# A fused attention, MLP and gated-MLP kernel: the first two blocks' 4-byte attention loads whole blocks, transposes its weights and keeps running sums; constant products stand ahead of all, and conversions 1 to 6 behind attention's steps

## The chip, the cores and the metric

One Trainium2 chip, one of its cores. The metric is the device time of one execution in microseconds (us); three runs of the kernel are given, and one execution was profiled. Engines by the names that the profile uses: PE (TensorE, PEld its weight loads), DVE (VectorE), ACT (ScalarE), POOL (GpSimd), SP (SyncE, which here issues most DMAs).

## The reference

Three stages in sequence. `q`, `k`, `v` are [4, 8, 576, 64] in float32, and `f` holds forget gates per position. Cut to what is computed:

```python
scores = (q @ k^T) / 8
cum    = cumsum(log(clip(f, 1e-4, 1)))
scores = where(causal, -1e9, scores + cum[:, :, :, None] - cum[:, :, None, :])
attn   = exp(scores - max);  attn /= sum(attn) + 1e-9
x      = (attn @ v), heads merged to [4, 576, 512]
xn     = (x - mean) / sqrt(var + 1e-6) * g_ln
x      = x + relu(xn @ w_ch1) @ w_ch2            # hidden size 2048
h      = relu(x @ w_in);  u, v = halves of h
v_n    = (v - mean) / sqrt(var + 1e-6)
out    = (u * (w_spatial @ v_n + b_spatial)) @ w_out
```

The weights `w_ch1`, `w_ch2`, `w_in` and `w_out` are float64 and arrive as 8-byte words.

## The kernel before, in words

The rows of all batches (4 x 576) are cut into nine groups of 256 or fewer columns. `BLOCKS` lists the first eight as (batch, kind). Blocks 0 and 1 are kind 0: the first 128 rows of two batches each, whose attention has one 128x128 tile per head, done in 4-byte products by `attention32`. Blocks 2 and 3 are kind 1 (rows 128 to 255, `attention1`), the other four kind 2. Each block's attention yields xT, 512 features by 256 columns; `norm` subtracts the mean and forms the scale y; `mlp` runs the two products with the hidden size cut into 16 pieces j. Block 0's MLP (g = 0) works in 4-byte products with the converted weights as they are; the later ones use pairs of 2-byte halves that `make16` cuts out of the same weights once their scale is known (`squares`, `scales`).

Converting a weight piece (`load_w`, `narrow`, lines 509 to 519 and 480 to 501): `load_raw` (503) brings 1 MB of 8-byte words into one of two buffers `raw`; ScalarE forms the magnitude of the high word (495, into wt) and the scaled low word (496, into low); VectorE clamps (497), merges the sign (498, which reads raw too) and joins both (499). The next piece but one can be loaded when the ScalarE steps and line 498 are through. `PACE` holds back the magnitude step of a conversion until attention's step number `done[...]` has had its weights copied out of PSUM (348), for later conversions until a ReLU of the MLP. `RAWAT` and `CONV` are the positions on the plan's time axis at which raw loads and conversions are recorded.

`attention32` (308) handles a block in four steps p of four heads (two batches n, two heads u). Per step it loads the operands qk (two rows of decays, line 323, and two transfers of q and k, 325) and the values vr (326); TensorE forms the scores (332) into a PSUM bank; VectorE adds the mask and takes the minimum of the negated scores (335); ScalarE takes the exponential with its sum (337); VectorE turns the reciprocal sums into a diagonal matrix (343) and TensorE multiplies the weights with it (347), which transposes and scales at once; ScalarE copies the result (348); TensorE multiplies with the values (353), ScalarE copies them into xT (354). `norm` then forms the mean over the 512 features as four products with a matrix of ones and the mean of squares as four more where it gets no running sum s (577 to 605); the other blocks come with a running sum.

Every engine works through its own queue in order. The order is made by a scheduler from the recorded sequence, buffers and priorities; it is not written out by hand. SyncE's queue, through which most loads go, is one of them: a load that waits for its buffer holds back all loads behind it.

## Time and profile before

| | us |
|---|---|
| three runs | 810.55, 814.67, 816.39 |
| their median | 814.67 |
| the profiled execution | 813.44 |
| its span, first to last instruction | 811.7 |

Times in the profile count from the start of the span. Busy time is the time in which an engine works on an instruction. A 4-byte product shows as two MATMUL records. In a row of the timeline the first two numbers are start and duration, x is the number of records merged, and the bracket tells how long the engine was idle before and what released it. In a row of windows each engine has its busy time and its number of instructions, then come the granted TensorE clock (1.00 is 2.4 GHz, 0.50 is 1.2 GHz), the share of the DMA engines that was busy and the GB/s.

### The profile page before, as it was taken

How to read it: one execution, taken by the hardware profiler on the slowest of the kernel's cores; microseconds unless marked ns; L12 is line 12 of the kernel's file. 1: busy time of each engine (PE TensorE's matmuls, PEld its weight loads, DVE VectorE, ACT ScalarE, POOL GpSimd, SP SyncE). 2: the span in 40 equal slices, each digit the busy share in tenths (PEclk: the TensorE clock that was granted, in tenths of full speed). 3: DMA queues.
4: the chain of work that ended last, by engine and by line, in shares of the span. 5: the costliest groups of instructions: out<-in, count | busy, mean ns of one | idle time of the engine just before them, and what ended most of it. 6: DMA issues, size and time to landing. Idle time of an engine off the chain costs nothing.

```text
span 811.7 us, 16139 instructions
## 1 busy us (share of the span) xinstructions
PE 765.0 (94%) x5868; PEld 583.7 (72%) x5868; DVE 553.6 (68%) x1495; ACT 526.9 (65%) x1319; POOL 55.0 (7%) x83
## 2 busy tenths in 40 slices
PE   1799989899999999999999999999999999999997
PEld 1688878678887878788778888644447667667676
DVE  5657985788598979768876963778435663664734
ACT  4676876988499869658776962576325644656542
POOL 3000000110200110101011100100012000000000
PEclk9989999999999999999999999999999999999999
DMA  6558993765668995985795875651024230000101
GB/s 187 178 176 269 251 264 75 202 155 102 165 163 168 220 205 111 178 187 125 177 193 133 140 113 147 159 174 52 1 43 81 66 117 1 30 31 5 55 1 59
DMA packets 166066, 104.71 MB, mean 129 GB/s; under 512 B 106402, under 2 KB 153634, under 8 KB 165988
## 3 DMA queue, kind: packets, MB, share of 16 engines
q1 hardware_dynamic: 159800, 97.19, 48.4%
q0 software_dynamic: 5184, 4.72, 4.6%
q10 hardware_dynamic: 1004, 1.78, 0.7%
q8 instruction: 46, 0.75, 0.4%
q14 instruction: 32, 0.26, 0.1%
HBM read 64.37 MB, written 15.11 MB: 98 GB/s over the span
## 4 chain that ended last, share of the span: by engine, by line
PE 62%; DMA 15%; ACT 9%; DVE 9%; issue 3%; SPq 2%; POOL 0%; DVEq 0%; ACTq 0%; POOLq 0%
PE ph L666 13%; PE acc L651 12%; PE pb L607 8%; PE pb L608 8%; PE pb L609 8%; DMA PT<-P 5%; DMA raw<-in_moe_w_ch_dram 4%; PE av L427 3%; PE s L281 3%; DMA qk<-in_qk_dram 2%; DVE P L302 1%; PE s L651 1%; DVE sd L285 1%; ACT wt L559 1%; DMA vr<-in_v_dram 1%
## 5 line engine op out<-in xcount | busy, mean ns | idle before, releaser
L651 PE MATMUL acc<-hh,wt 128*128 128x256 f16 (+2 forms) x960 | 198.2, 298 | 2.6 <-ACT hh L671 2.6
L666 PE MATMUL ph<-xh,wt 128*128 128x256 f16 (+1 forms) x896 | 185.5, 289 | 4.1 <-DVE hl L675 4.0
L666 PEld LDWEIGHTS <-wt 128*128 128x128 f16 x1344 | 127.4, 98 | 49.2 <-issue 10.2
L651 PEld LDWEIGHTS <-wt 128*128 128x128 f16 x1344 | 129.5, 99 | 45.8 <-issue 6.8
L666 PE MATMUL ph<-xl,wt 128*128 128x256 f16 (+1 forms) x448 | 129.1, 288 | 0.0
L651 PE MATMUL acc<-hl,wt 128*128 128x256 f16 (+1 forms) x416 | 116.4, 284 | 0.0
L671 ACT ACTIVATE hh<-ph 128x256 f16<-128x256 f32 (+2 forms) x128 | 51.1, 399 | 45.2 <-PE ph L666 44.7
L246 ACT ACTIVATE P<-sd,st 128x512 f16<-128x512 f32 (+2 forms) x128 | 70.8, 587 | 8.3 <-DVE st L292 5.2
L675 DVE SCALAR_TENSOR_TENSOR hl<-ph,hh 128x256 f16<-128x256 f32 (+1 forms) x112 | 50.7, 454 | 37.1 <-ACT hh L671 36.7
L289 ACT ACTIVATE sd<-sd,st 128x384 f32<-128x384 f32 (+2 forms) x80 | 54.7, 684 | 21.9 <-DVE st L285 21.3
L302 DVE SCALAR_TENSOR_TENSOR P<-sd,st,P 128x384 f16<-128x384 f32 (+2 forms) x96 | 58.9, 632 | 8.4 <-ACT P L246 6.9
L281 PE MATMUL s<-x 68*128 68x384 f32 (+7 forms) x256 | 61.2, 356 | 1.3 <-DMA x<-decay_d 0.8
L696 POOL DMA_DIRECT2D x_d<-t x36 | 32.4, 1104 | 333.7 <-DVE t L692 178.0
L285 DVE CUSTOM_DVE_ANT_0 sd<-s,mask 128x384 f32<-128x384 f32 (+2 forms) x80 | 45.7, 580 | 7.7 <-PE s L281 6.8
L246 ACT ACTIVATE x<-qk 64x320 fp32r<-64x320 f32 (+1 forms) x64 | 41.6, 697 | 2.1 <-PE s L281 1.6
L281 PEld LDWEIGHTS s<-x 68*128 68x128 f32 (+3 forms) x256 | 37.7, 177 | 3.5 <-PE s L281 1.0
L427 PE MATMUL av<-PT,vp 128*64 128x320 f16 (+2 forms) x480 | 34.9, 274 | 5.2 <-DMA PT<-P 5.2
L947 DVE SCALAR_TENSOR_TENSOR u<-pb,wsc,u 128x288 f32<-128x288 f32 x32 | 15.9, 514 | 32.9 <-PE pb L946 32.9
L607 PE MATMUL pb<-x2h,wil 128*128 128x288 f16 (+2 forms) x144 | 37.9, 273 | 0.0
L608 PE MATMUL pb<-x2l,wih 128*128 128x288 f16 (+2 forms) x144 | 37.9, 273 | 0.0
L609 PE MATMUL pb<-x2h,wih 128*128 128x288 f16 (+2 forms) x144 | 37.9, 273 | 0.0
L427 PEld LDWEIGHTS <-vp 128*64 128x64 f16 (+1 forms) x480 | 24.8, 110 | 17.2 <-issue 10.7
(273 smaller groups left out, 1616.3 us busy)
## 6 DMA issues: line engine op xcount, KB each, us to landing
raw<-in_moe_w_ch_dram SPq DMA_DIRECT2D x32, 512.0 KB
qk<-in_qk_dram SPq DMA_DIRECT2D x32, 448.0 KB
vraw<-in_v_dram SPq DMA_DIRECT2D x5, 1024.0 KB
vr<-in_v_dram SPq DMA_DIRECT2D x16, 320.0 KB
x_d<-xT SPq DMA_DIRECT2D x9, 512.0 KB
x_d<-t POOLq DMA_DIRECT2D x36, 128.0 KB, 4.7
out_dram<-o SPq DMA_DIRECT2D x32, 144.0 KB
raw<-in_moe_w_in_dram SPq DMA_DIRECT2D x8, 512.0 KB
```

The lines of the kernel that those rows point to most:

```text
L246: self.nc.scalar.activation(out, in_, AF.Copy, scale=scale)
L281: nc.tensor.matmul(ps[: R * u + R, : c1 - c0], lhsT=x[:, lo - q0 - R * u : hi - q0], rhs=y[:, c0:c1], start=g == 0, stop=g == len(heads[u] ...
L285: nc.vector.tensor_tensor_reduce(out=sd[:M, c0:c1], in0=ps[:M, : c1 - c0], in1=mask, scale=-0.125, scalar=3e38 if n == 0 else st[:M, n - 1 ...
L289: nc.scalar.activation(sd[:M, :N], sd[:M, :N], AF.Exp, bias=st[:M, n : n + 1], scale=-1.0, accum_out=st[:M, 2:3])
L302: nc.vector.scalar_tensor_tensor(out=dl, in0=src, scalar=rs, in1=dh, op0=ALU.mult, op1=ALU.subtract)
L427: nc.tensor.matmul(pav[us, n0:W], lhsT=vp[:kr, vi, kt, us], rhs=heads[u][1][:kr, 2 * kt + pi, n0:W], start=(kt == 0 and (vi, pi) == (0, 1) ...
L607: first = mm(out, lhsT=al, rhs=bh, start=start, stop=False, **kw)
L608: mm(out, lhsT=ah, rhs=bl, start=False, stop=False, **kw)
L609: mm(out, lhsT=ah, rhs=bh, start=False, stop=stop, **kw)
L651: ins = nc.tensor.matmul(acc[m], lhsT=a, rhs=b, start=bank not in clear, stop=last and e == len(terms) - 1, skip_group_check=True)
L666: nc.tensor.matmul(ph, lhsT=a, rhs=b, start=k == e == 0, stop=k == NK - 1 and e == len(terms) - 1)
L671: relu = nc.scalar.activation(hh, ph, AF.Relu)
```

## The change

`attention32` loads a block's operands and values whole: two transfers for q and k, two for the decays and one for the values, where four steps had five each; both have one buffer where there were two. The weights are scaled on VectorE in place and then transposed on TensorE against the identity; the values are multiplied in two products of 256 columns, and the two halves of the result are copied by ScalarE and VectorE. The steps are recorded so that the values of a step follow the weights of the next. The block's running sum is formed on the way, and `norm` always takes one. 48 products of constants are recorded ahead of all. `PACE` now has seven entries and holds back both ScalarE steps of conversions 1 to 6. The forget gates are loaded in plain order of heads, so the rows by which decays are addressed change in all attentions.

```diff
-BUFS0 = dict(vr=2, qk=2, e=3, diag=2, PT=2, st=4)
+BUFS0 = dict(vr=1, qk=1, e=3, PT=2, st=4)
+WARM = 48
-RAWAT = (-1.1, -1.1)
+RAWAT = (-0.97, -0.97)
-PACE = (None, None, 2, 5, 7)
+PACE = (None, 0, 1, 2, 4, 6, 7)
...
-        for p in range(NP):
-            qk = at.tile([66, 2, 2, 2 * P], F32, tag="qk", name="qk", bufs=bufs["qk"])
-            vr = at.tile([P, 2, P], F32, tag="vr", name="vr", bufs=bufs["vr"])
...
+        qk = at.tile([66, 2, NP, 2, 2 * P], F32, tag="qk", name="qk", bufs=bufs["qk"])
+        vr = at.tile([P, 2, DM], F32, tag="vr", name="vr", bufs=bufs["vr"])
+        for n in range(2):
+            nc.sync.dma_start(out=qk[:64, n].rearrange("d p u s -> d p (u s)"), in_=self.qk0[b + n].rearrange("p d u s -> d p (u s)"))
+        for r in range(2):
+            nc.sync.dma_start(out=qk[64 + r : 65 + r].rearrange("r n p u s -> r (n p u) s"), in_=self.decay[b * H : b * H + 16, r])
+        nc.sync.dma_start(out=vr, in_=self.v[b : b + 2, :P, :].rearrange("b p d -> p b d"))
...
+            nc.vector.tensor_tensor(out=flat, in0=flat, in1=st[:, 1].unsqueeze(2).broadcast_to([P, 4, P]), op=ALU.mult)
...
-                mm(ps[:, n, u], lhsT=e[:, n, u], rhs=diag[:, n, u], start=True, stop=True, skip_group_check=True)
+                nc.tensor.transpose(ps[:, n, u], e[:, n, u], self.ident)
...
-                for u in (1, 0):
-                    mm(pav[: 64 * u + 64, 0, n], lhsT=vr[:, n, : 64 * u + 64], rhs=pt[:, n, u], start=True, stop=True, skip_group_check=True)
-            nc.scalar.activation(xT[:, p].rearrange("p (n w) -> p n w", n=2), pav[:, 0], AF.Copy)
+                mm(pav[:, n], lhsT=vr[:, n, p * P : (p + 1) * P], rhs=pt[:, n], start=True, stop=True, skip_group_check=True)
+            for u in range(2):
...
+                if u:
+                    nc.scalar.activation(dst, pav[us, :, u], AF.Copy)
+                else:
+                    nc.vector.tensor_copy(out=dst, in_=pav[us, :, u])
+            if p == 1:
+                self.xs = self.mo_sum(xT)
+            elif p == 2:
+                nc.vector.tensor_tensor(out=self.xs, in0=self.xs, in1=xT[:, 2, :], op=ALU.add)
...
         at = PACE[j] if j < len(PACE) else 2 * NP + j - len(PACE)
         if at is not None:
-            self.after(first, self.done[at])
+            for ins in first if j < len(PACE) else first[:1]:
+                self.after(ins, self.done[at])
...
-        if s is None or end:
+        if end:
             pv = self.mean(tag, *(sq[:, t] for t in range(NK)))
...
+        warm, ones = self.bank("s2"), self.ones.bitcast(BF16)
+        for i in range(WARM):
+            self.nc.tensor.matmul(warm[:, : 2 * P], lhsT=ones[:, :P], rhs=ones, start=True, stop=True)
```

Three places show what this moves. The first is SyncE's queue at the start of the program, before (ft are the gates, raw_150 and raw_153 the weight pieces 0 and 1, qk_157 and vr_158 the operands and values of the first step):

```order
L148 DMA ft_96<-in_f_dram 16x1x576
L507 DMA raw_150<-in_moe_w_ch1_dram 128x4x128
L508 DMA raw_150<-in_moe_w_ch2_dram 128x512
L507 DMA raw_153<-in_moe_w_ch1_dram 128x4x128
L508 DMA raw_153<-in_moe_w_ch2_dram 128x512
L325 DMA qk_157<-in_qk0_dram 64x2x256
L323 DMA qk_157<-decay_100 1x4x256 x2
```

and after, with qk_200 and vr_201 the operands and values of the whole first block and raw_207 and raw_210 pieces 0 and 1:

```order
L149 DMA ft_145<-in_f_dram 16x576
L323 DMA qk_200<-in_qk0_dram 64x4x512 x2
L326 DMA vr_201<-in_v_dram 128x2x512
L529 DMA raw_207<-in_moe_w_ch1_dram 128x4x128
L530 DMA raw_207<-in_moe_w_ch2_dram 128x512
L325 DMA qk_200<-decay_149 1x16x256 x2
L180 DMA decay1_d_67<-dec1_150 32x768
L529 DMA raw_210<-in_moe_w_ch1_dram 128x4x128
```

The block's operands and values went ahead of the raw pieces, and piece 1 behind the decays.

The second place is SyncE's queue later in these two blocks. Before, the values of the second block's steps (vr_351, vr_399, vr_447, vr_486) stand between pieces 4 and 5 (raw_535, raw_571):

```order
L507 DMA raw_535<-in_moe_w_ch1_dram 128x4x128
L326 DMA vr_351<-in_v_dram 128x2x128
L508 DMA raw_535<-in_moe_w_ch2_dram 128x512
L326 DMA vr_399<-in_v_dram 128x2x128
L1025 DMA x2_d_70<-xT_156 128x4x256
L507 DMA raw_571<-in_moe_w_ch1_dram 128x4x128
L326 DMA vr_447<-in_v_dram 128x2x128
L508 DMA raw_571<-in_moe_w_ch2_dram 128x512
L326 DMA vr_486<-in_v_dram 128x2x128
```

After, qk_379 and vr_380 are the second block's operands and values, and raw_369 to raw_666 are pieces 2 to 6:

```order
L530 DMA raw_369<-in_moe_w_ch2_dram 128x512
L323 DMA qk_379<-in_qk0_dram 64x4x512 x2
L325 DMA qk_379<-decay_149 1x16x256 x2
L529 DMA raw_452<-in_moe_w_ch1_dram 128x4x128
L530 DMA raw_452<-in_moe_w_ch2_dram 128x512
L529 DMA raw_527<-in_moe_w_ch1_dram 128x4x128
L530 DMA raw_527<-in_moe_w_ch2_dram 128x512
L529 DMA raw_562<-in_moe_w_ch1_dram 128x4x128
L530 DMA raw_562<-in_moe_w_ch2_dram 128x512
L326 DMA vr_380<-in_v_dram 128x2x512
L529 DMA raw_666<-in_moe_w_ch1_dram 128x4x128
```

The second block's operands stand behind piece 2, its values behind piece 5.

The third place is ScalarE's queue where the MLP of block 0 begins (sq is the square for the norm, xT<-xT,gT the scaling of the MLP's operand, hh the first ReLU). Before, conversions 4 and 5 are raw_535 and raw_571:

```order
L495 ACTIVATE wt_146<-raw_437 128x1024
L337 ACTIVATE e_493,st_495<-e_493,st_495 128x128 x4
L354 ACTIVATE xT_349<-s_392 128x256
L587 ACTIVATE sq_324<-xT_156 128x1024
L348 ACTIVATE PT_472<-ph_471 128x512
L338 ACTIVATE st_495<-st_495 128x4
L630 ACTIVATE xT_156<-xT_156,gT_64 128x256 x4
L354 ACTIVATE xT_349<-s_431 128x256
L496 ACTIVATE low_574<-raw_571 128x1024
L595 ACTIVATE y_314<-av_326,eps_65 128x256
L348 ACTIVATE PT_511<-ph_510 128x512
L495 ACTIVATE wt_146<-raw_535 128x1024
```

After, raw_666 is piece 6, raw_708 piece 7 and raw_770 piece 8:

```order
L352 ACTIVATE PT_507<-ph_506 128x512
L518 ACTIVATE wt_195<-raw_666 128x1024
L518 ACTIVATE low_669<-raw_666 128x1024
L607 ACTIVATE sq_345<-xT_199 128x1024
L360 ACTIVATE xT_378<-s_468 64x256
L650 ACTIVATE xT_199<-xT_199,gT_64 128x256 x4
L518 ACTIVATE low_711<-raw_708 128x1024
L360 ACTIVATE xT_378<-s_500 64x256
L518 ACTIVATE low_773<-raw_770 128x1024
L691 ACTIVATE hh_560<-ph_555 128x256
L518 ACTIVATE wt_195<-raw_708 128x1024
```

Conversion 6 stands ahead of the MLP's operand where conversion 3 stood, and the low words of pieces 7 and 8 ahead of the first ReLU.

## Rows read from the trace of the kernel before

**Rows 1.** The page's busy time, share of the span and instructions of each engine.

```profile
PE 765.0 (94%) x5868; PEld 583.7 (72%) x5868; DVE 553.6 (68%) x1495; ACT 526.9 (65%) x1319; POOL 55.0 (7%) x83
```

**Rows 2.** Windows of the whole core: the program's five stages, each engine's busy time.

```profile
14.40:31.20 16.80, 11.72 (x48) 10.57 (x49) 10.84 (x43) 9.43 (x36) 0.00 (x0) 1.00 0.60 167
31.20:59.30 28.10, 25.32 (x146) 20.43 (x146) 16.02 (x53) 20.90 (x64) 0.00 (x0) 0.88 0.59 186
59.30:145.10 85.80, 82.35 (x533) 70.40 (x533) 64.61 (x152) 63.47 (x141) 0.00 (x0) 0.98 0.77 213
145.10:171.00 25.90, 21.72 (x183) 17.64 (x182) 19.85 (x42) 25.82 (x52) 3.73 (x4) 0.93 0.63 166
171.00:811.70 640.70, 623.86 (x4966) 464.57 (x4964) 435.39 (x1189) 400.97 (x1020) 44.81 (x60) 0.99 0.50 111
```

**Rows 3.** Waits of PE in 59.3 to 145.1 us: total, times, longest.

```profile
PE av L399 <- DMA PT<-P: 3.5, 2, 3.0
```

**Rows 4.** Timeline of PE, 14 to 78 us.

```profile
14.39 2.04 PE L332 MATMUL acc<-qk 66*128 66x128 f32 x8 [14.39 <-DMA qk<-decay]
36.96 1.14 PE L332 MATMUL s<-qk 66*128 66x128 f32 x8 [2.19 <-DMA qk<-in_qk_dram]
37.92 2.57 PE L353 MATMUL av<-PT,vr 128*128 128x128 f32 x8
53.32 1.16 PE L347 MATMUL ph<-diag,e 128*128 128x128 f32 x8
59.35 1.89 PE L666 MATMUL ph<-xT,wt 128*128 128x256 f32 x8
61.08 1.53 PE L353 MATMUL s<-PT,vr 128*128 128x128 f32 x8
62.54 3.72 PE L666 MATMUL ph<-xT,wt 128*128 128x256 f32 x16
66.09 1.89 PE L651 MATMUL acc<-hh,wt 128*128 128x256 f32 x8
74.99 2.92 PE L529 MATMUL gram<-wt 128*128 128x128 bf16 x48
77.75 0.33 PE L212 MATMUL s<-vq,ones 128*128 128x1 f32 x2
```

**Rows 5.** Windows: 2 to 14.4 us, last column GB/s.

```profile
2.00:14.40 12.40, 0.01 (x1) 0.04 (x1) 6.62 (x15) 6.30 (x10) 5.02 (x13) 1.00 0.80 237
```

**Rows 6.** Timeline of ACT, 50 to 63 us.

```profile
50.50 1.17 ACT L496 ACTIVATE low<-raw 128x1024 int32<-128x1024 uint32 x1 [0.46 <-DMA raw<-in_moe_w_ch_dram]
53.06 0.43 ACT L337 ACTIVATE e<-e,st 128x128 f32<-128x128 f32 x1
54.61 0.41 ACT L354 ACTIVATE xT<-s 128x256 f32<-128x256 f32 x1
54.87 1.09 ACT L587 ACTIVATE sq<-xT 128x1024 f32<-128x1024 f32 x1
56.39 1.74 ACT L630 ACTIVATE xT<-xT,gT 128x256 f32<-128x256 f32 x4
```

**Rows 7.** Timeline of DVE, 0 to 56 us.

```profile
1.04 0.17 DVE L131 MEMSET ones<- 128x128 f32 x1
16.59 0.29 DVE L335 CUSTOM_DVE_ANT_0 e<-acc,mask 128x128 f32<-128x128 f32 x1 [0.66 <-PE acc L332]
51.70 1.22 DVE L498 SCALAR_TENSOR_TENSOR low<-raw,low 128x1024 uint32<-128x1024 uint32 x1 [0.72 <-ACT low L496]
54.17 0.68 DVE L497 TENSOR_SCALAR wt<-wt 128x1024 f32<-128x1024 f32 x1
54.88 1.22 DVE L499 SCALAR_TENSOR_TENSOR wt<-wt,low 128x1024 uint32<-128x1024 uint32 x1
```

**Rows 8.** The chain that ended last: start, us, what.

```profile
46.32 4.10 DMA raw<-in_moe_w_ch_dram
```

**Rows 9.** Windows: 38 to 40 us.

```profile
38.00:40.00 2.00, 2.00 (x8) 1.22 (x8) 2.00 (x9) 2.00 (x7) 0.00 (x0) 0.50 0.32 95
```

More of the change, by code (lines that the diff above doesn't have):

```diff
@@ L147, in decays @@
         for c, queue in ((0, nc.sync), (2 * H, nc.scalar)):
-            queue.dma_start(out=ft[c : c + 2 * H], in_=self.f[c : c + 2 * H].rearrange("(n h) s -> h n s", n=2))
+            queue.dma_start(out=ft[c : c + 2 * H], in_=self.f[c : c + 2 * H])
         nc.scalar.preload_act_table_set("natural_log_exp_and_others")
@@ L348, in attention32 @@
[L348 to L355 removed]
+            flat = e.rearrange("p n u w -> p (n u) w")
+            nc.vector.tensor_tensor(out=flat, in0=flat, in1=st[:, 1].unsqueeze(2).broadcast_to([P, 4, P]), op=ALU.mult)
@@ new lines, in weights, with values @@
+            return e
+        def values(p, e):
+            ps, pt = bank(tags[1]), four("PT")
+            for n, u, c in four_:
+                nc.tensor.transpose(ps[:, n, u], e[:, n, u], self.ident)
+            self.done.append(nc.scalar.activation(pt, ps, AF.Copy))
+            pav = bank(tags[2])
+            for n in range(2):
+                mm(pav[:, n], lhsT=vr[:, n, p * P : (p + 1) * P], rhs=pt[:, n], start=True, stop=True, skip_group_check=True)
+            for u in range(2):
+                us = slice(64 * u, 64 * u + 64)
+                dst = xT[us, p].rearrange("p (n w) -> p n w", n=2)
+                if u:
[6 more added lines that the diff above has]
+                nc.vector.tensor_tensor(out=self.xs, in0=self.xs, in1=xT[:, 2, :], op=ALU.add)
@@ L358, in attention1 @@
+        late = None
+        for p in range(NP):
+            e = weights(p)
+            yield
+            if late:
+                values(*late)
+                yield
+            late = p, e
+        values(*late)
+        yield
+        return self.xs
     def attention1(self, b, xT):
@@ L493, in narrow @@
         else:
-            first = nc.scalar.activation(a, words(raw, 1, F32), AF.Abs, scale=2.0**16)
-            nc.scalar.activation(low.bitcast(I32), lo, AF.Copy, scale=LOW)
+            first = [nc.scalar.activation(a, words(raw, 1, F32), AF.Abs, scale=2.0**16), nc.scalar.activation(low.bitcast(I32), lo, AF.Copy, scale=LOW)]
             nc.vector.tensor_scalar(out=a, in0=a, scalar1=F64_LO * 2.0**16, scalar2=F64_HI * 2.0**16, op0=ALU.max, op1=ALU.min)
@@ L577, in norm @@
         tag = "s" if end else "av"
-        if s is None:
-            pm = self.mean(tag, *(x[:, t] for t in range(NK)))
-        else:
-            nc.vector.tensor_tensor(out=s, in0=s, in1=x[:, 3, :], op=ALU.add)
-            pm = self.mean(tag, s)
+        nc.vector.tensor_tensor(out=s, in0=s, in1=x[:, 3, :], op=ALU.add)
+        pm = self.mean(tag, s)
         for t in range(NK):
@@ L1037, in prep @@
                 yield
-        steps = [(NP * 3, NP * 6, NP * 8 + 1)[kind] + 3 for _, kind in BLOCKS] + [4]
+        steps = [(NP * 2 + 1, NP * 6, NP * 8 + 1)[kind] + 3 for _, kind in BLOCKS] + [4]
         events = []
```

31 lines of the change are left out of this document (9 added, 22 removed).

## The prediction

> **What bounds the kernel now.** I read four views in this order. First the engine shares: TensorE is busy 94% of the span, VectorE 68%, ScalarE 65% [rows 1]. Such an average says nothing of one stage, so I cut the span where the program changes its work [rows 2]. The change touches only the first two stages and the front of the third: the scores of the first two blocks (14.4 to 31.2 us), the rest of their attention (to 59.3), and the first hidden layer with 4-byte weights (59.3 to 145.1), in which all 16 weight pieces are converted. In the first two, no engine is full: VectorE works 10.84 + 16.02 = 26.9 us of 44.9 (60%), ScalarE 30.3 (68%). That is a chain of steps that wait for one another. In the third stage TensorE is busy 82.35 of 85.80 us, and the waits view has one releaser for it, the transposing DMAs of the next block, 3.5 us [rows 2, 3]. So what counts is when TensorE gets to the first product of the hidden layer (59.35 us) [rows 4] and how much work stands behind that point. From 145.1 on ScalarE takes over until 171 (25.82 of 25.90 us) with the scaling of the weights; it starts on a product that stands near the end of the third stage, so it moves with that stage. Behind that the order on every engine is as before, but for a swap or two, and a shift at 145 reaches the end.
>
> **The change part by part.** Own time of the profiled execution: 813.44 us, span 811.7; the median of the runs is 814.67, 1.2 above it.
>
> *Loads.* Ahead of the first scores SyncE's queue had both raw weight pieces, a quarter of the block's operands and the decays. Now it has, by the shapes, all operands of the block (1.05 MB), its values (0.52), raw piece 0 (1.05), and behind these the two decay rows. With the two loads on ScalarE's queue (0.26) and the gates (0.07) that is 2.95 MB ahead of them. From 2.0 to 14.4 us the queues moved 237 GB/s, which is 2.94 MB [rows 5]. So the decays land at 14.4 again: 0 us. The thirty DMAs fewer (5 instead of 20 for each block) cost some 0.6 us of SyncE each, but SyncE is waited for only where it feeds a buffer; I count them at nothing.
>
> *First reduction.* VectorE has the first step of conversion 0 ahead of the first mask-and-minimum. Raw piece 0 lands with the decays, ScalarE's half takes 1.17 and VectorE's 1.22: 14.4 + 2.4 = 16.8 instead of 16.59 [rows 6, 7]. +0.2 us.
>
> *Attention's work.* VectorE's count up to the point at which block 0's mean is subtracted: the 26.9 us of before, plus two more of each of the first two conversion steps and one more of the third (conversions 0 to 5 instead of 1 to 4, by their part): 2 x 1.22 + 2 x 0.68 + 1.22 = 5.0 [rows 7]; five copies of halves out of PSUM, at most the 0.41 that ScalarE's whole copies take [rows 6]: 2.0; three running sums at about 0.4: 1.3. Sum 35.2 us. It starts at 15.6 with conversion 0, so without a single wait it ends at 50.8, and with the 40% idle of before at 15.6 + 35.2 / 0.60 = 74. Neither end is near; I take the waits by name. (a) The second block's values now have one buffer, which the first block's last product frees, and their load stands behind raw piece 5 in SyncE's order (second place shown). I put that product at 43 to 44, from ScalarE's rows ahead of it (28 exponentials of at most 0.43, 7 conversion halves at 1.1 [rows 6], 5 copies and small ones that I put at 3: some 23 us of work from 17 on) and 3 to 4 us of waits. Issue 0.6 and a landing like that of half a raw piece on a free queue (4.10) [rows 8] give 48.5. ScalarE reaches the copy that needs it (the transposed weights have two buffers) at about 47: with the product itself, 3.6 us lost. (b) TensorE's order puts the last transposes behind that product, 2 us more. (c) Some 2 us for the arrival of the second block's operands and single hand-overs. So 50.8 + 7.6 = 58.4; the square (1.09) stands ahead of the scaling of the operand (a quarter of 1.74) on ScalarE [rows 6], and with the hand-overs that is 1.9 more: the hidden layer's first product at 60.3, against 59.35. +1.0 us.
>
> *Transposes instead of products with a diagonal.* The four 128x128 products of a step (8 records) took 1.16 us [rows 4]; transposes cost between nothing and the same. The scaling moves from the diagonal to the weights, 128x512 on VectorE either way. TensorE waits in this stage, so 0 us at either end.
>
> *Work behind the first hidden product.* In the third stage TensorE had 8 products for means (16 records) and two steps of values (2 x 1.46 us, from 61.08 to 62.54). A record of 256 columns takes (66.09 - 62.54) / 16 = 0.222 us [rows 4]. Now there are 3 products for means (6 records, 1.3 us instead of 3.5) and one step of values in two products (0.9 instead of 2.9); a remnant of 0.2 goes too. -4.4 us. GpSimd's sums that replace the products of block 0 feed only its scale, which is used at the MLP's end.
>
> *Conversions ahead.* ScalarE now has the low words of conversions 7 and 8 ahead of the first ReLU of the hidden layer (third place shown). Piece 8 needs the buffer that conversion 6 leaves: after 58.4 VectorE has four more steps, so about 61.9; second half issued at 62.4, landed 4.1 later, converted 1.17, ReLU 0.4: 68.0. TensorE has then done the two groups of products that fit into its two banks and the odd ones: 60.3 + 16 x 0.222 + 1.3 = 65.1. It waits 3.0 us, which also hides a half clock at the start of the stage. +3.0 us. Bounds: 0 (piece 8 there in time) and 6. From there conversions run two steps further ahead of the products than before; TensorE waited for no conversion in that stage [rows 3], so I give nothing for it.
>
> *48 products of constants.* They can begin when the ones are written (1.2 us) [rows 7]. Other 2-byte products of half the columns come (77.75 - 74.99) / 48 = 0.0575 us apart; twice that for 256 columns and twice again at half the clock is 0.23, so all end by 12.3, and TensorE had nothing to do before 14.39 [rows 4]. Cost 0. Then it is idle for 2 us or more. In this trace an idle of 2.19 us was followed by the granted clock 0.50, the 1.2 GHz level, and by 2.57 us for eight records that take 1.53 later [rows 4, 9]. So I give them no gain; the bound is the 1 us by which the first group of eight (2.04) exceeds a later one (1.14), twice.
>
> Sum: +0.2 (inside the 1.0) gives +1.0 - 4.4 + 3.0 = -0.4 us: 813.0 from the profiled execution, 814.3 from the median. I take 813.6. A measurement of this kernel tells about 1%, 8 us, from no change.
>
> **The rivals.** *It gets faster.* If the named waits mostly vanish (operands and values in time, VectorE 90% full), the first hidden product comes at 15.6 + 35.2 / 0.90 + 1.9 = 56.6 to 55, that is -3.5; with -4.4, no wait for piece 8, and the 3.5 us on the transposing DMAs halved because conversions are out of their way: -9.7, 803.7. For it: VectorE and ScalarE keep 75% and 74% in the third stage [rows 2], where conversions and attention also share them. Against: single buffers where there were two.
>
> *It gets slower.* TensorE stays at the half clock through attention. Its work there shrinks (values from 1.46 to 0.9 us a step, transposes cheaper) while a step takes VectorE 35.2 / 8 = 4.4, so it idles more than before, and a fall to 0.50 needed no more than the idle of 2.19 us above. Then the serial end (values, transposes, values, values of the second block, 0.9 us each) doubles, +3.6, the first block's scores +2, and the hidden layer's first groups +3.5 of which the wait for piece 8 hides little, since that slides too: together +9, so 822. It decides when the granted clock is under 1.00 for most of 40 to 65 us. The Trainium skill speaks for this rival: "TensorE: Matmul & The Clock Gate", Part 4: PE-mode transpose, says that transposes do not count as activity that releases the clock. No run here has shown a transpose yet; by that rule the sum would be this rival's.
>
> *The pacing does nothing* (conversions were not in attention's way): then only the sum's other terms stand, -4.4 and +1.0, 810; this is inside the forecast's range.
>
> **How the numbers follow.** Forecast (within 1%) 0.62; faster rival 0.20; slower rival 0.18. The likeliest case alone runs from 808 to 818. Range: the low end from the earliest start (50.8 + 1.9 = 52.7, -6.6, with -4.4 gives 802.4), the high end 822; with one tenth left out on either side 804 to 821.
>
> **What would show it.** Right: the first hidden product near 60 us with conversions 0 to 6 done; an idle TensorE for the second block's values near 45 to 49 and for the first ReLU near 65 to 68; the third stage, from first hidden product to its last, some 84 us. Wrong towards faster: no such idle and the first hidden product before 57. Wrong towards slower: granted clock near 0.5 over 40 to 65, or the first product after 64. That anything behind 171 us changes by more than 2 us would refute the view that the rest only shifts.

## The result, and the profile after

The changed kernel takes 821.04 us (median of 4 runs, 818.88 to 824.54) where the kernel before, on the same chip, takes 812.61: a ratio of 1.011, 95% interval 1.006 to 1.016. It is slower by some 1.1%, and the interval does not reach 1. The profiled execution took 821.27 us, with a span of 819.6.

The page's line of busy times answers to [rows 1]:

```profile
PE 760.2 (93%) x5828; PEld 580.3 (71%) x5828; DVE 560.7 (68%) x1509; ACT 528.4 (64%) x1319; POOL 60.6 (7%) x87
```

TensorE has 4.8 us less to do and the span is 7.9 us longer: the time is in waits. The windows of the same kernel, cut at the points that answer to [rows 2, 5] (the columns are start, end, length, then busy time of PE, PEld, DVE, ACT and POOL with their instructions, the granted clock, the DMA share and GB/s):

```profile
2.00:14.40 12.40, 6.81 (x46) 5.14 (x44) 5.46 (x14) 3.93 (x8) 5.74 (x13) 0.92 0.97 246
14.40:31.20 16.80, 10.95 (x44) 9.69 (x44) 12.19 (x45) 11.84 (x41) 0.00 (x0) 0.55 0.71 203
31.20:69.40 38.20, 19.44 (x83) 15.36 (x84) 26.84 (x71) 26.14 (x65) 2.17 (x2) 0.70 0.60 176
69.40:153.10 83.70, 79.71 (x509) 68.26 (x508) 59.93 (x149) 58.25 (x134) 2.87 (x2) 0.95 0.69 191
153.10:819.60 666.50, 642.56 (x5148) 481.32 (x5146) 455.92 (x1230) 427.52 (x1073) 48.41 (x64) 1.00 0.51 113
```

Attention's second stage grew from 28.1 us [rows 2] to 38.2, and no engine is full in it: VectorE works 26.84 us of it, ScalarE 26.14. The hidden layer with 4-byte weights shrank from 85.8 to 83.7, and all behind it is as long as it was. The point that separates the two is the first product with 2-byte weights, here the start of the first of the products from `xh` (after the median durations, the times of the first and the last), before and after:

```profile
L666 PE MATMUL ph<-xh,wt x896: 269/273/421, 145.0 to 595.6; 128*128 128x256 f16 x154, 128*128 128x512 f16 x26
```

```profile
L686 PE MATMUL ph<-xh,wt x896: 269/273/421, 153.2 to 605.1; 128*128 128x256 f16 x154, 128*128 128x512 f16 x26
```

It comes 8.2 us later, and from it to the span's end it takes 666.4 us, against 666.7 before. So the whole loss is made by 153 us, and in fact by 69. Where, the waits of TensorE show (14 to 70 us of the kernel after; total, times, longest):

```profile
PE s L335 <- DMA qk<-decay: 8.6, 1, 8.6
PE acc L335 <- DMA qk<-decay: 7.9, 1, 7.9
PE s L355 <- ACT xT L360: 6.4, 2, 4.2
PE av L593 <- DVE ls L601: 2.9, 1, 2.9
PE av L355 <- ACT xT L360: 1.7, 2, 1.1
```

The second line is the wait for the first block's operands, which is hidden behind nothing in either kernel. The first is new: TensorE stands 8.6 us for the *second* block's decay rows. Its timeline (start, us, what, and in brackets the idle time before it and what ended it):

```profile
16.73 7.17 PE L335 MATMUL acc<-qk 66*128 66x128 f32 x32 [7.92 <-DMA qk<-decay]
...
25.89 2.07 PE L355 MATMUL av<-PT,vr 128*128 128x256 f32 x4 [1.14 <-ACT PT L352]
27.76 1.06 PE L351 MATMUL ph<-ident,e 128*128 128x128 f32 x4
37.39 3.76 PE L335 MATMUL s<-qk 66*128 66x128 f32 x16 [8.57 <-DMA qk<-decay]
...
55.88 0.67 PE L593 MATMUL av<-ls,onesf 128*128 128x256 f32 x2 [2.86 <-DVE ls L601]
56.44 1.69 PE L355 MATMUL s<-PT,vr 128*128 128x256 f32 x4
...
61.25 2.07 PE L355 MATMUL s<-PT,vr 128*128 128x256 f32 x4 [2.27 <-ACT xT L360]
67.48 2.08 PE L355 MATMUL s<-PT,vr 128*128 128x256 f32 x4 [4.16 <-ACT xT L360]
69.35 1.06 PE L686 MATMUL ph<-xT,wt 128*128 128x256 f32 x2
```

The hidden layer's first product comes at 69.35 us, against 59.35 [rows 4]. SyncE's queue says why the second block is late:

```profile
22.98 0.37 SPq L529 DMA_DIRECT2D raw<-in_moe_w_ch_dram  x1
23.40 0.50 SPq L530 DMA_DIRECT2D raw<-in_moe_w_ch_dram  x1
24.01 2.40 SPq L323 DMA_DIRECT2D qk<-in_qk_dram  x2
26.46 1.24 SPq L325 DMA_DIRECT2D qk<-decay  x2
29.18 0.38 SPq L529 DMA_DIRECT2D raw<-in_moe_w_ch_dram  x1
...
52.61 0.37 SPq L326 DMA_DIRECT2D vr<-in_v_dram  x1
```

With one buffer for a block's operands, their load must wait for the first block's last score (16.73 + 7.17 = 23.90); it goes at 24.01, behind raw piece 2, and raw piece 3 follows it. Two windows of the same kernel show what the queues did:

```profile
18.00:23.00 5.00, 5.00 (x25) 5.00 (x25) 3.97 (x26) 3.70 (x15) 0.00 (x0) 0.50 0.13 52
23.00:37.40 14.40, 4.69 (x18) 3.44 (x16) 9.66 (x23) 9.63 (x30) 0.00 (x0) 0.62 0.90 225
```

They stood nearly empty (52 GB/s) for the five us in which the second block could have been loaded, and then had three things at once: 225 GB/s for 14.4 us is 3.2 MB, two raw pieces and the operands. Behind the waiting score, in TensorE's order, stood the first block's own values of steps 1 to 3. For steps 1 and 2 VectorE and ScalarE had done their part (the weights of step 1 were transposed and copied by 30.0 us, those of step 2 scaled by 31.3); for step 3 they had not, since in VectorE's own order the scaling of its weights stood behind the mask and minimum of the waiting scores, and ran at 41.46.

### The profile page after: what moved, and what is told of

Same layout as the page of the kernel before. It is cut to its first block, busy times and chain, and to the rows that moved or that the text cites. A ratio compares the mean times of both kernels' runs of the same rounds, so it can differ in the third digit from the quotient of the medians.

```text
span 819.6 us, 16030 instructions
## 1 busy us (share of the span) xinstructions
PE 760.2 (93%) x5828; PEld 580.3 (71%) x5828; DVE 560.7 (68%) x1509; ACT 528.4 (64%) x1319; POOL 60.6 (7%) x87
## 4 chain that ended last, share of the span: by engine, by line
PE 53%; DMA 16%; DVE 13%; ACT 11%; issue 3%; SPq 2%; DVEq 0%; ACTq 0%
PE ph L686 10%; PE acc L671 9%; PE pb L627 8%; PE pb L628 8%; PE pb L629 7%; DMA PT<-P 5%; PE av L450 3%; DMA raw<-in_moe_w_ch_dram 3%; DMA qk<-decay 2%; DMA qk<-in_qk_dram 2%; PE s L282 2%; DMA x_d<-xT 2%; ACT wt L582 2%; DVE P L303 1%; PE s L671 1%
## 5 line engine op out<-in xcount | busy, mean ns | idle before, releaser
L627 PE MATMUL pb<-wsh,vl 128*128 128x288 f16 x128 | 36.6, 286 | 0.2 <-DVE x2s L200 0.2
```

The source lines that it names most:

```text
L627: first = mm(out, lhsT=al, rhs=bh, start=start, stop=False, **kw)
```

## Experiments

Each kernel was timed in rounds with the kernel before on one chip (ratios with 95% intervals are to that). From its profile I read two points: the hidden layer's first product and the first 2-byte product, which before are 59.35 and 145.0, after 69.35 and 153.2. The second is the better one, since some of these kernels order hidden products and values otherwise. Medians less that point are 666 to 671 us in all sixteen kernels. The first hidden product has two of the second block's four steps of values ahead of it in the kernel before, in qk2, vr2, raw2late and pace, three in the kernel after, in bufs2, order3, prod, nowarm, dec0, order3b, order3bprod and sums, and all four in bufs2prod and b2prodpace. Both points are read from one execution each, and executions of one kernel differ: those profiled for vr2 and sums were the fastest of their ten (809.02 and 807.40 us, medians 814.99 and 811.64). A microsecond or two between two kernels' points is therefore not told apart. The intervals of bufs2 and of the kernels built on it lie clear below that of the kernel after, and that of raw2late touches it; those of qk2, vr2, order3 and prod overlap it, so what these four give back is read from the points and the medians and is less certain.

| kernel | first hidden product | first 2-byte product | ratio to before | interval |
|---|---|---|---|---|
| after | 69.35 | 153.2 | 1.0110 | 1.0060 to 1.0159 |
| bufs2: two buffers each | 60.88 | 145.9 | 1.0003 | 0.9972 to 1.0035 |
| qk2: operands only | 58.85 | 146.1 | 1.0051 | 1.0016 to 1.0086 |
| vr2: values only | 60.44 | 143.9 | 1.0041 | 1.0008 to 1.0073 |
| raw2late | 61.98 | 147.1 | 1.0025 | 0.9990 to 1.0060 |
| order3 | 68.68 | 148.5 | 1.0061 | 1.0024 to 1.0098 |
| prod | 66.26 | 150.0 | 1.0076 | 1.0043 to 1.0108 |
| pace | 65.04 | 153.4 | 1.0104 | 1.0056 to 1.0151 |
| nowarm | 69.92 | 155.0 | 1.0150 | 1.0089 to 1.0211 |
| dec0 (on bufs2) | 60.51 | 147.9 | 1.0017 | 0.9985 to 1.0048 |
| order3b (on bufs2) | 62.07 | 143.5 | 0.9995 | 0.9956 to 1.0035 |
| bufs2prod (on bufs2) | 59.94 | 142.4 | 0.9981 | 0.9948 to 1.0014 |
| order3bprod (on bufs2) | 64.16 | 143.4 | 0.9997 | 0.9961 to 1.0032 |
| b2prodpace (on bufs2prod) | 60.08 | 140.5 | 0.9932 | 0.9901 to 0.9964 |
| sums (on before) | 59.51 | 143.2 | 0.9991 | 0.9956 to 1.0027 |

### Four theories of the loss

The theories are late loads (A), the half clock from the transposes (B), conversions in the way of attention's copies (C), and some effect of the 48 products of constants.

**bufs2.** `BUFS0 = dict(vr=1, qk=1,` becomes `vr=2, qk=2,`.

> The kernel after, with two buffers instead of one for the 4-byte attention's operands and values, so that the second block's loads need not wait for the first block's last products. Theory A (late loads: in the kernel after the second block's operands are issued at 24.0 us, behind the first block's last score, and its first score starts at 37.39, after 8.57 us of idle TensorE; its values are issued only at 52.6): these loads go out before 20 us, the second block's scores follow the first block's work with no wait of over 2 us for decay rows, and the hidden layer's first product, at 69.35 in the kernel after, comes at 58 to 62; the time falls by 7 to 10 us, to a ratio of 0.998 to 1.003 against the kernel before. Theory B (TensorE at half clock through attention because of the transposes): granted clock stays under 0.85 from 40 to 65 us and the first product comes at 65 or later; ratio 1.005 to 1.011. Theory C (the conversions stand ahead of attention's copies on ScalarE): TensorE's waits for ScalarE's copies of xT (6.4 us) stay, the first product comes at 63 to 66; ratio 1.003 to 1.008.

Theory A holds: the loads go out early, the second block's scores follow at 25.26 us, and the loss is gone (1.0003). TensorE's timeline and a window of this run:

```profile
16.25 7.17 PE L335 MATMUL acc<-qk 66*128 66x128 f32 x32 [6.75 <-DMA qk<-decay]
23.21 1.91 PE L351 MATMUL ph<-ident,e 128*128 128x128 f32 x8
25.26 3.75 PE L335 MATMUL s<-qk 66*128 66x128 f32 x16
...
60.88 5.79 PE L686 MATMUL ph<-xT,wt 128*128 128x256 f32 x16 [3.27 <-ACT xT L650]
```

```profile
18.00:23.00 5.00, 5.00 (x26) 5.00 (x26) 3.82 (x28) 4.15 (x21) 0.00 (x0) 0.50 1.06 264
```

The same five us now carry 264 GB/s instead of 52. The half clock, theory B's cause, is still there (granted 0.67, 0.67 and 0.50 from 40 to 65 us, where the kernel after has 0.84, 0.84 and 0.50; 16 records of hidden products take 5.79 us instead of [rows 4]'s 3.72), and the time is nevertheless back: the clock is not the main cause.

**prod.** The transpose becomes a product with the identity: `mm(ps[:, n, u], lhsT=e[:, n, u], rhs=self.ident, ...)`.

> The kernel after, with each transpose of attention's weights made by a product with the same identity (the same four 128x128 operations a step, as ordinary products). Theory A (late loads): the granted clock may rise, but the second block's scores still begin at about 37 and the first hidden product still comes at 68 to 70; ratio to the kernel before 1.008 to 1.012, as for the kernel after. Theory B (half clock from transposes): the granted clock is above 0.95 over 40 to 65 us instead of 0.84, 0.84 and 0.50, and the first hidden product comes 3 to 6 us earlier, at 63 to 66; ratio 1.003 to 1.007. Theory C (conversions on ScalarE): as A.

Theory B is right that the clock rises (0.80, 1.00 and 0.94 from 40 to 65 us, where it asked for more than 0.95 throughout) and may have a part of the loss: first hidden product and first 2-byte product come 3.1 and 3.2 us earlier, while the ratio, 1.0076, is not told apart from that of the kernel after. Some of that is the second block's operands, which came 2.1 us earlier in this execution (35.27). The windows of the kernel after and of this one, 40 to 60 us:

```profile
40.00:50.00 10.00, 7.53 (x42) 6.36 (x40) 9.26 (x34) 9.21 (x34) 0.00 (x0) 0.84 0.31 105
50.00:60.00 10.00, 5.30 (x22) 3.63 (x22) 6.70 (x20) 7.01 (x17) 0.00 (x0) 0.84 0.62 159
```

```profile
40.00:50.00 10.00, 6.86 (x39) 6.22 (x38) 7.68 (x25) 6.25 (x24) 0.00 (x0) 0.80 0.51 166
50.00:60.00 10.00, 6.48 (x40) 5.14 (x38) 8.69 (x21) 8.34 (x18) 0.00 (x0) 1.00 0.77 229
```

**pace.** Conversions held back nearly as before:

```diff
-PACE = (None, 0, 1, 2, 4, 6, 7)
+PACE = (None, None, 2, 4, 7)
-            for ins in first if j < len(PACE) else first[:1]:
+            for ins in first[:1]:
```

> The kernel after, with conversions 2 to 6 held back as in the kernel before: 2 behind attention's step 2, 3 behind step 4, 4 behind step 7, from 5 on behind the hidden layer's ReLUs, and with only the first of a conversion's two ScalarE operations held. Theory C (conversions in attention's way on ScalarE and VectorE): three conversions less in attention, at 2.2 us of ScalarE and 3.1 of VectorE each, and the first hidden product comes 5 to 8 us earlier, at 61 to 64; the hidden layer gives back 2 to 3 by waiting for its weights; ratio to the kernel before 1.003 to 1.007. Theory A (late loads): the second block's operands still wait for the first block's last score, its first score begins at 34 to 37, and the first hidden product comes at 66 to 69; ratio 1.008 to 1.012. Theory B (half clock): as A, with a clock as low as in the kernel after.

The first hidden product came 4.3 us earlier, with one more step of values moved behind it, and nothing of it was left at the first 2-byte product (153.4): the hidden layer took 88.4 us instead of 83.9. With the loads late, earlier conversions cost nothing on balance, and theory C falls as a cause of the loss.

**nowarm.** `WARM = 0`.

> The kernel after without the 48 products of constants ahead of all. All theories: the first block's scores start at 16.7 us as with them, at the same granted clock of about 0.5 (TensorE was idle for 7.92 us between the constants and the scores), 32 records in 7.2 us, and the first hidden product at 69.35 within 1 us; ratio to the kernel after 0.998 to 1.002. If the constants do release the clock for attention, the scores take longer or the clock over 14 to 50 us is lower than in the kernel after, and the time rises by 2 us or more; if they cost something, the loads or the first score come earlier by up to 1 us.

Up to the first hidden product it is the kernel after, within 0.6 us; the constants show neither gain nor cost there. The ratio is not told apart from that of the kernel after; the 1.2 us more that it lost by 155 us in the profiled execution, and 7 more behind that, I did not trace to this edit.

### Which load, and why it costs so much

**qk2** and **vr2.** Two buffers for one of the two: `vr=1, qk=2` and `vr=2, qk=1`.

> The kernel after, with two buffers for the 4-byte attention's operands alone; its values keep one. It splits the gain of the run with two buffers for both (first hidden product 60.88 us instead of 69.35, ratio to the kernel before 1.000 instead of 1.011). If the late operands are the whole of it: second block's first score at about 25 us, first hidden product at 60 to 62, ratio 0.999 to 1.002. If the late values weigh as the prediction had them (3.6 us and 2 behind them): the second block's values are issued when the first block's last product is done, near 48, land 4 to 5 us later, where the run with two buffers has its first product with them at 43.0; the first hidden product then comes at 64 to 67, ratio 1.004 to 1.008.

> The kernel after, with two buffers for the values alone; the operands keep one. If the late operands are the cause: second block's first score at 37 us as in the kernel after, first hidden product at 67 to 70, ratio to the kernel before 1.008 to 1.012. If the late values are: first hidden product at 63 to 65, ratio 1.003 to 1.006.

Both first hidden products come earlier than expected; both ratios lie where the account of the late values put them. By these figures each alone takes back half of the loss or more: 0.6% and 0.7% of 1.1% by the ratios, 7.1 and 9.3 of 8.2 us by the first 2-byte product. So the two don't add. For qk2 the reason was the expected one (second block's scores at 25.05, its values issued at 48.70). vr2 contradicts the simple theory: its operands are nearly as late as in the kernel after (35.57 against 37.39), where the late values had cost TensorE only 0.3 us of waiting, and yet the first hidden product comes at 60.44:

```profile
25.78 2.08 PE L355 MATMUL av<-PT,vr 128*128 128x256 f32 x4 [0.44 <-ACT PT L352]
30.35 2.08 PE L355 MATMUL av<-PT,vr 128*128 128x256 f32 x4 [2.50 <-ACT xT L360]
32.22 1.06 PE L351 MATMUL ph<-ident,e 128*128 128x128 f32 x4
35.57 3.75 PE L335 MATMUL s<-qk 66*128 66x128 f32 x16 [2.29 <-DMA qk<-decay]
...
60.44 1.89 PE L686 MATMUL ph<-xT,wt 128*128 128x256 f32 x8
```

TensorE's idle time before that score is 2.29 us instead of 8.57, since other work stands ahead of it. The number of buffers had also changed the order that the scheduling makes, so a run that alters a buffer must be read with the order beside it. (In bufs2 and qk2, too: there the second block's first scores stand ahead of all of the first block's values.) Of the kernel after and of vr2 (av the first block's values, s2 the second block's scores):

```
after                                    vr2
L351 MATMUL ph_249<-ident_83,e_214       L351 MATMUL ph_249<-ident_83,e_214
L355 MATMUL av_256<-PT_250,vr_201        L351 MATMUL ph_279<-ident_83,e_232
L351 MATMUL ph_279<-ident_83,e_232       L355 MATMUL av_256<-PT_250,vr_201
L335 MATMUL s2_386<-qk_379               L355 MATMUL av_286<-PT_280,vr_201
L335 MATMUL s2_404<-qk_379               L351 MATMUL ph_311<-ident_83,e_262
L351 MATMUL ph_311<-ident_83,e_262       L335 MATMUL s2_386<-qk_379
L355 MATMUL av_286<-PT_280,vr_201        L335 MATMUL s2_404<-qk_379
```

So the loss has two factors: the load is late, and what doesn't need it stands behind the instruction that waits for it. The next two runs were made to take one factor each; the scheduling moved other work as well, as noted with each.

**raw2late.** Arrival: single buffers, raw piece 2 behind the second block's operands (the new value in `CONV` only records piece 2 after them).

```diff
+            self.dec = nc.sync.dma_start(out=qk[64 + r : 65 + r]...
+        for load in loads if j == 2 else ():
+            self.after(load, self.dec)
-CONV = (-0.6, -0.59, -0.58, -0.38, -0.14)
+CONV = (-0.6, -0.59, -0.57, -0.38, -0.14)
```

> The kernel after, single buffers kept, with raw weight piece 2 behind the second block's operands and decay rows in SyncE's queue instead of ahead of them. In the kernel after the operands could go at 24.0 us (first block's last score) and the first score of the second block came at 37.39, while raw pieces 2 and 3 and the operands moved 3.1 MB. Theory A1 (the transfers share the queues, and the pieces ahead cost the time): with 1.05 MB alone at 237 GB/s the operands land at 28 to 31 and the score starts there, 6 to 9 us earlier; first hidden product at 62 to 66; ratio to the kernel before 1.003 to 1.008. Rival A2 (the decay rows, 16 KB into one partition, take about 10.9 us from their issue whatever is ahead of them: issued 5.85 and landed 16.7 for the first block, issued 26.5 and landed 37.4 for the second): the score starts at 35 to 37, first hidden product at 67 to 69, ratio 1.008 to 1.011.

```profile
24.97 1.24 SPq L325 DMA_DIRECT2D qk<-decay  x2
26.32 0.52 SPq L529 DMA_DIRECT2D raw<-in_moe_w_ch_dram  x1
```

```profile
32.52 3.75 PE L335 MATMUL s<-qk 66*128 66x128 f32 x16 [4.06 <-DMA qk<-decay]
...
61.98 2.99 PE L688 MATMUL ph<-xT,wt 128*128 128x256 f32 x8
```

4.9 us earlier, between the two accounts: the decay rows landed 6.3 us after the end of their issue instead of 9.7, not after a constant time, so what shares the queues counts; they still had the operands ahead of them, and pieces 2 and 3, issued at 26.32 and 28.82, beside them. The first hidden product moved by 7.4 us, more than the score did, because TensorE's order changed with the load: a step of the second block's values moved behind it, and the first block's values of step 1 stand right behind the first two steps of scores. The first 2-byte product came 6.1 us earlier. So a load in another place in the queue, with the order that follows from it, gives back most of the loss (1.0025) without a byte of buffer.

**order3.** Order: single buffers, SyncE's queue as it is up to the second block's values, the second block's first score behind the first block's last values (`self.after(score, self.v1)`).

> The kernel after, single buffers and SyncE's queue as they are; only TensorE's order is changed: the second block's first score stands behind the first block's last product with values (in the kernel after, the scores of its steps 0 and 1 stand ahead of the first block's values 1 to 3). Theory A (late operands hold back what is queued behind them on TensorE): the operands come as late as before, first score of the second block at 34 to 38 us, but the first block's values no longer wait for it: its last values are done near 38 instead of 52.4, its mean product by 42 instead of 55.9, and the first hidden product comes at 56 to 61 instead of 69.35; ratio to the kernel before 0.999 to 1.004. Rival (the late operands by themselves, or ScalarE's conversions, set the end): first hidden product at 66 to 70, ratio 1.008 to 1.012.

Neither account: ratio 1.0061, some half of the loss back (the interval overlaps that of the kernel after), but the first hidden product only at 68.68. The values ended at 46, not at 38; they waited for ScalarE's copies (6.1 us in three waits). The longest, 3.5 us, was for a copy that in ScalarE's order stood behind the conversion of piece 3, and ScalarE stood 4.13 us for that piece, until 38.48: there, too, work waits behind an instruction that waits for a load. The second block's scores, now at 46.02, were late themselves, and the scheduling moved VectorE's and ScalarE's work on them back with them. The gain shows behind: with much of attention's work done, the hidden layer took 79.8 us.

**dec0** (on bufs2): raw piece 0 behind the first block's decay rows, and conversion 0 behind step 0 (`PACE = (0, 0, 1, ...)`). Half of the second block's operands moved up into its place, so there is half a MB less ahead.

> The kernel with two buffers for operands and values, with raw weight piece 0 behind the first block's decay rows in SyncE's queue instead of ahead of them, and conversion 0 held behind attention's step 0. Theory A1 (volume ahead in the queues): 2.4 MB instead of 2.95 ahead of the decay rows, and the first score comes at 12 to 14 us instead of 16.25; the first hidden product at 56 to 59 instead of 60.88; ratio to the kernel before 0.994 to 0.998. Rival A2 (the decay rows take 10.9 us from issue whatever is ahead): first score at 16 or later. Rival: the raw pieces, 4 us later now, become what is late, and the first hidden product stays at 60 to 62, ratio 0.999 to 1.002.

The first score came 0.8 us earlier (15.47), and that was lost again; the last rival stands. The loads ahead of the first score are not worth an edit.

**sums** (on before): only the running sums of the first two blocks.

> The kernel before with one part of the change alone: the first two blocks' sums for the mean are kept running on VectorE, so that the mean takes one product instead of four, and the first block's squares are summed on GpSimd (one product instead of four). By the prediction's count that is 6 products of 2 records at 0.222 us for each block less 0, that is 12 products of means and variances less in all for both blocks, 24 records, 5.3 us of TensorE, of which those behind the first hidden product (59.35 us) count: 2 to 4 us. First hidden product at 58 to 60, the third stage (85.65 us from first hidden product to the first 2-byte product) 81.5 to 83.5; ratio to the kernel before 0.995 to 0.998. Rival (TensorE's freed time is taken by waits for conversions and copies): stage 85 to 86, ratio 0.999 to 1.002.

First hidden product as before, first 2-byte product 1.8 us earlier, in the fastest of ten executions; the stage took 83.7 us, just outside the 81.5 to 83.5 that the count gave, and the timing shows nothing (0.9991).

### What is left when the loads are in time

**order3b** (bufs2 and order3) and **bufs2prod** (bufs2 and prod).

> The kernel after with both: two buffers for operands and values, and TensorE's order with the first block's values ahead of the second block's scores. If late loads and the order are two ways to the same loss, nothing is left to gain from the second: first hidden product within 2 us of that with the order alone, ratio to the kernel before 0.997 to 1.002. If each has a loss of its own: 3 us or more earlier than either alone (below 57), ratio 0.992 to 0.997.

> The kernel after with two buffers for operands and values, and ordinary products with the identity instead of transposes. Theory B, now as a second-order price: with transposes the second buffers leave the granted clock at 0.67 from 30 to 60 us, and each step of values and transposes takes 1.5 us more than at full clock; with products the clock over 30 to 60 us rises to 0.8 or more, and the first hidden product comes 2 to 4 us earlier than 60.88; ratio to the kernel before 0.996 to 0.999. Rival (VectorE and ScalarE set the pace of a step): clock up, first hidden product within 1 us of 60.88, ratio 1.000 to 1.003.

In the times, order has nothing measurable left once the loads are early (0.9995). With ordinary products the granted clock over 40 to 60 us is 0.92 and 0.93 instead of bufs2's 0.67, and the first 2-byte product comes at 142.4 instead of 145.9; the ratios' intervals overlap.

**order3bprod** (all three) and **b2prodpace** (bufs2prod with `PACE = (None, 0, 1, 2, 4)`, so that conversions 5 and 6 wait for the hidden layer's ReLUs).

> The kernel after with three changes: two buffers for operands and values, the first block's values ahead of the second block's scores on TensorE, and ordinary products with the identity instead of transposes. If the half clock (granted 0.50 to 0.67 over 14 to 60 us with buffers and order alone) is what is left on the path: first 2-byte product 2 to 3 us earlier than the 143.5 us of the run with buffers and order, at 140.5 to 141.5; ratio to the kernel before 0.994 to 0.998. If VectorE and ScalarE, both busy over 96% from 30 to 52 us with buffers and products, are what is left: 142.5 to 144, ratio 0.997 to 1.001.

> The kernel with two buffers for operands and values and ordinary products with the identity, with conversions 5 and 6 taken out of attention again (behind the hidden layer's first two ReLUs, as in the kernel before). In the run with buffers and products VectorE was busy 21.24 of 22 us from 30 to 52, ScalarE 21.19. If the engines' work is now the bound of attention: 6.2 us of VectorE and 4.4 of ScalarE less ahead of the first hidden product, which comes 3 to 6 us earlier than 59.94, at 54 to 57; the first 2-byte product at 138 to 141 unless the hidden layer waits for its weights; ratio to the kernel before 0.993 to 0.997. If the hidden layer then waits for these conversions: first hidden product earlier, first 2-byte product at 142 to 144, ratio 0.998 to 1.001.

order3bprod gained nothing over order3b, so products in place of transposes are not always a gain. b2prodpace is faster than the kernel before, 808.36 us against 812.11, 0.9932 (0.9901 to 0.9964), and so than the kernel after. Its first hidden product did not move as expected (60.08; products of weight pieces for the scales now fill TensorE ahead of it), but the first 2-byte product came at 140.5. The windows from 30 to 52 us of bufs2prod and of b2prodpace:

```profile
30.00:52.00 22.00, 17.11 (x89) 13.75 (x88) 21.24 (x62) 21.19 (x58) 0.00 (x0) 0.84 0.56 195
```

```profile
30.00:52.00 22.00, 15.48 (x76) 11.91 (x75) 20.23 (x56) 19.58 (x56) 0.00 (x0) 0.84 0.60 205
```

With the loads in time VectorE and ScalarE are full over these 22 us in bufs2prod (97% and 96%; before 54% and 69%, after 69% and 64%): only now can early conversions cost something. That moving two of them away is what makes the difference between these two is likely but not settled, as their intervals overlap.

## Why the prediction was wrong

The forecast was 813.6 us, no change; the kernel came out slower, at 821.04, just past the range's end of 821. Point by point:

- *Attention's work*: this is the step that failed, in its waits. It put the first hidden product at 60.3; it came at 69.35. The work was about right: VectorE was busy some 39 us from 15.6 to 69.4 (12.19 + 26.84 in two windows), conversion 6 (3.1 us) included; the step had 35.2 without it. The waits were put at 7.6 us, and VectorE idled some 15. Of them (c), "some 2 us for the arrival of the second block's operands and single hand-overs", measured 8.57 us of standing TensorE for the arrival alone. It was a round number and not a walk along SyncE's queue: the one buffer is free at 23.9, piece 2 is ahead and piece 3 behind, and 3.2 MB at the 237 GB/s of [rows 5] take 13.5 us from piece 2's issue at 23, which gives 36.5; it was 37.39. The bytes, the order and the rate stood ahead of the run; the moment would have had to be worked out from the scores. Nor did the step look at what TensorE has behind the waiting score: the last product with the first block's values, put at 43 to 44, came at 51.45, and with it wait (a) slid, from a landing at 48.5 to an issue at 52.61; since all on TensorE was late by then, it waited 0.3 us for these values, not 3.6. (a) named the right queue and the wrong tile. That the single buffers, by the late loads and the order that goes with them, were the cause is shown by bufs2 (8.5 of the 10.0 us at the first hidden product, and the whole of the time); that the place of one load is enough for most of it, by raw2late. That the order has a share of its own is seen in the points of order3 and vr2, and the times leave its size open.
- ScalarE's part of the same step: its copies of xT stood behind both halves of conversions 5 and 6, and TensorE waited 6.4 us for them. The timeline of ScalarE after (`low` and `wt` the two halves, `sq` the square):

```profile
63.92 1.13 ACT L518 ACTIVATE wt<-raw 128x1024 f32<-128x1024 f32 x1
64.94 1.14 ACT L518 ACTIVATE low<-raw 128x1024 int32<-128x1024 uint32 x1
65.96 1.07 ACT L607 ACTIVATE sq<-xT 128x1024 f32<-128x1024 f32 x1
67.05 0.38 ACT L360 ACTIVATE xT<-s 64x256 f32<-64x256 f32 x1
```

  The prediction's third place showed this order, but the step charged 1.9 us for all that ScalarE does there. In pace, with these conversions gone, 2.5 us of such waits stayed, and the hidden layer gave the gain back.
- *Loads*, 0: the first score came at 16.73, not 14.39, though the queues moved 246 GB/s instead of 237. The sum counted the 2.95 MB ahead of the decays; by 16.7 us the queues had moved 3.8 MB (258 GB/s over 14.7 us), as piece 1, issued behind the decays at 11.42, ran beside them. dec0 shows that half a MB less ahead is worth 0.8 us; how the rest divides is open. *First reduction* then came at 18.93 instead of 16.8, later by about as much.
- *Transposes*, 0: probably missed. The points of prod put them, with the clock, at up to 3.2 us, of which the earlier operands have a part.
- *Work behind the first hidden product* and *Conversions ahead*, -4.4 and +3.0: together -1.4, measured -1.8 (83.85 us from the first hidden to the first 2-byte product, 85.65 before). Right in sum, and that was luck: the wait for the first ReLU, the +3.0, is not there, as TensorE's waits from 69.4 to 153.1 us are 3.2 us for a scale of the next block's values (the line below) and 0.7 for a transposing DMA; and its busy time fell by 2.6 us (82.35 to 79.71), not by 4.4.

```profile
PE s L213 <- DVE vs L200: 3.2, 1, 3.2
```

- *48 products of constants*, 0: right up to the first hidden product, by nowarm's trace; the times leave open what they do behind it.
- That all behind 171 us only shifts: right, 666.4 us behind the first 2-byte product against 666.7.
- The slower rival named 822 and its condition was met: the granted clock was 0.84, 0.84 and 0.50 in the windows from 40 to 65 us. But its mechanism has 3.2 us at most of 8.2, and its +2 for the first block's scores was no loss, as these ran at 1.2 GHz in the kernel before too (last section). By the rule of the Trainium skill ("TensorE: Matmul & The Clock Gate", Part 4: PE-mode transpose), a transpose does not count as activity for the clock; prod agrees, with 1.00 instead of 0.84 from 50 to 60 us, yet in order3bprod, with ordinary products alone, the clock is 0.50 from 40 to 50 us at 90% busy (the window's row below). So it hung on more than the kind of product. (The faster rival's sign, a first hidden product before 57 us, did not come. That the pacing does nothing agrees with pace, 1.0104 against 1.0110, but that rival's 810 had the loads in time.)

```profile
40.00:50.00 10.00, 9.01 (x36) 8.36 (x36) 6.20 (x33) 5.39 (x22) 0.00 (x0) 0.50 0.45 156
```

## What to carry to other kernels

When loads are merged into larger ones and buffers are halved to pay for them, find for each buffer the last reader, and walk the DMA queue from that moment with the bytes that stand around the load: here 3.2 MB at the measured rate give the late arrival within 1 us. Then read, on every engine that will wait, what stands behind the waiting instruction and doesn't need it; as each engine here works in order, that work is late too. Here moving the load ahead of another load took back most of the loss, and moving the work ahead of the wait some of it. Work put early into idle time is free only as long as the engines idle for another reason: when the loads were in time, VectorE and ScalarE were full with the early conversions among their work, and taking two of them away probably paid.

## What the runs showed of the hardware that I had not expected

The clock column can read full where no clock was recorded. In nowarm it shows full clock from 14.4 us on, yet the 32 records of the first scores take as long as in the kernel after, at 0.50:

```profile
16.40:30.00 13.60, 10.94 (x44) 9.71 (x44) 11.26 (x44) 11.39 (x41) 0.00 (x0) 1.00 0.61 182
```

```profile
16.46 7.17 PE L335 MATMUL acc<-qk 66*128 66x128 f32 x32 [16.46 <-DMA qk<-decay]
```

With no products ahead, no change of the clock had been recorded yet, and the column seems to show full clock until one is. So the 1.00 of [rows 2] for 14.4 to 31.2 us was probably no reading either. The durations tell it: the first eight records in [rows 4] take 2.04 us where eight later ones take 1.14, so both kernels make their first scores at 1.2 GHz. The Trainium skill ("TensorE: Matmul & The Clock Gate", Part 1: The HAM clock gate, Seeing it yourself) warns that the trace's clock events on this chip have been seen to be unreliable; here the durations decided.
